# One more pair of weight chunks converted in place, and a planner that rests for two steps, in a banded attention with two feed-forward layers

## The chip, the cores and the metric

The kernel runs on one core of one Trainium2 chip. The metric is the device time of one execution in microseconds (us), from several runs; the trace comes from one more, profiled execution. Engines are named as the profile names them: PE is the matmul engine (TensorE), DVE is VectorE, ACT is ScalarE, POOL is GpSimd, and SP is the engine that issues most of the DMAs.

## What is computed

Attention with a band mask on q, k, v of shape (4, 8, 576, 64), then two feed-forward layers on the 2304 tokens of 512 features that come out of it, all in float32:

```python
scores = where(mask, q @ k.T / 8, -1e9)          # 32 keys back; dilated by 4 for half of the heads
x = softmax(scores) @ v                          # as (2304, 512)
h = x @ w_in                                     # 512 -> 2048
g = where(h > 0, h, exp(min(h, 0)) - 1)
x = g @ w_out                                    # 2048 -> 512
out = ((x @ w_a) * (x @ w_b)) @ w2_out           # 512 -> 1536 -> 512
```

The weights reach the chip as 64-bit floats, seen as pairs of 32-bit words, so every weight has to be put together on the chip before a matmul can use it.

## The kernel before

**Tiles and steps.** The tokens stand in six tiles of 384. The first layer's 2048 hidden features are 16 columns f of 128. A *step* is one pair (tile t, column f); `STEPS1` lists the 96 of them: steps 0 to 6 are tile 0 with f = 0 to 6, steps 7 to 22 are tile 1 with f = 0 to 15, steps 23 to 31 are tile 0 with f = 7 to 15, and from step 32 tiles 2 to 5 follow, 16 steps each. Behind the steps comes the second layer, by Strassen-like products (`ab_step`, lines L974 and L1290).

**One step** s issues `h1_mm(s)`: 12 matmuls into the PSUM tile ps_h (L525; two such buffers), then on ACT a Relu (L546) and an Exp (L547); `h1_g(s)`: on DVE the join of both (L552), which frees ps_h for step s + 2, on ACT the high part of g (L536), on POOL its low part (L537); and `y1_mm(s - 2)`: 12 matmuls from g into four tiles ps_y (L571). Every float32 product is three passes of a high and a low part. When a tile's last column is done (step 6 for tile 0's first part, step 22 for tile 1), two ACT copies (L608) and two DVE copies (L606) empty ps_y and free it for the next tile. The attention of a later tile runs between the steps, in slots of its own: scores (L474), softmax (L490, L356, L360, L369, L370), transposes (L499) with ACT copies (L502), values (L514), and the split of the result into x (ACT L462, DVE L463). Scores, transposes and values share two PSUM buffers, ps_a.

**Weights of the first layer.** Column f needs the chunk ("1i", f) for h1 and ("1o", f) for y1, 128 x 512 weights each. A chunk is a DMA of 512 KB into a buffer wraw (four of them), and then: ACT L252 (high word), ACT L257 (low word), DVE L262, L267 and L270 (clamp, join, sign), ACT L278 (high part), DVE L297 or L854 (low part). There are two ways to issue this. `w_convert` does it in place ("inline"), a pair of chunks at a time, in slot "C" of one step; `w_load` issues the DMAs a step ahead. This is done for the columns f below `SPLIT` = 7. For the rest, `chunk_ops` puts the same operations into a list that the planner works off.

**The planner.** `tick()` is called twice per step, once in slot "C" and once as a half-step in the next step's slot "A0". Each tick adds an allowance per engine (`ROOM1` for its first 32 ticks: 1.8 us of DVE and 1.4 of ACT; then `ROOM`) and issues from the head of the list whatever is ready: its inputs were issued enough ticks ago, a buffer is free, and the allowance is not used up. Behind the chunks of the first layer stand the second layer's weights in the same list (`unit_ops`: assembly, sums L917, low parts L901, high parts L278, and DMAs to DRAM, L829). Which instruction stands where on an engine is then settled by the tile framework from the order of issue and its dependences; at run time each engine works through its own list in order.

The place where the two ways part, and the loop that sets the ticks:

```python
    for f in range(NF1):                                             # L1394
        ...
        if f >= SPLIT:                                               # L1397
            for k in ks[::-1]:
                chunk_ops(k)
            continue
        ...
        at_step(st, "C", w_convert, ks, "w", ON1)                    # L1404
...
    for st in range(C1, NS1 - 3):                                    # L1461; C1 = 7
        same = st < C0 or STEPS1[st - 2][0] == STEPS1[st - 1][0]
        at_step(st, "C" if same else "C2", tick)
        at_step(st + 1, "A0", tick, True)
```

Of the kernel before, what the change touches and what calls it, by code (L numbers as in the profile page):

```python
# [36 lines left out]
SPLIT = 7  # L37
# [25 lines left out]
ON0, ON1 = "AAV", "AAV"  # L63
# [152 lines left out]
def banded_attention_two_ffn(ctx: ExitStack, tc: tile.TileContext, ins, out):  # L216
# [626 lines left out]
    def chunk_ops(key):  # L843

        at = {}
        x = assembly(at)(key)

        def hi():
            at["to"] = pools["wb"].tile([128, 2, 512], F32R, tag="w", name="w")
            part_hi("A", at["to"][:, 0, :], at["t", key])  # L850

        def lo():
            w = w_sb[key] = at["to"]
            V.tensor_tensor(w[:, 1, :], at["t", key], f32(w[:, 0, :]), op=SUB)  # L854

        give("wraw", x)
        give("wt", Op("V", 512, lo, Op("A", 512, hi, x)))
# [464 lines left out]
    def at_step(step, slot, fn, *args):  # L1322
        todo.setdefault((step, slot), []).append((fn, args))
# [70 lines left out]
    for f in range(NF1):  # L1394
        st = f
        ks = [("1o", f)] + ([("1i", f + 2)] if f + 2 < NF1 else [])
        if f >= SPLIT:  # L1397
            for k in ks[::-1]:
                chunk_ops(k)
            continue  # L1400
        for k in ks:
            if k != ("1o", 0):
                at_step(max(0, st - 1), "B" if f else "L", w_load, k)
        at_step(st, "C", w_convert, ks, "w", ON1)  # L1404


    def held(fn, *args):
# [51 lines left out]
    for j in range(FP):  # L1459
        unit_ops(j)  # L1460
    for st in range(C1, NS1 - 3):  # L1461
        same = st < C0 or STEPS1[st - 2][0] == STEPS1[st - 1][0]
        at_step(st, "C" if same else "C2", tick)
        at_step(st + 1, "A0", tick, True)
# [113 lines left out]
```

## Time and profile before

| | us |
|---|---|
| median of 3 runs | 916.57 (915.07 to 921.31) |
| profiled execution | 915.85 |
| its span, first to last instruction | 914.0 |
| mean granted clock of PE | 0.998 of full speed |

Idle time in the span counts only on the engine that sets the end. In a timeline row the first number is the start in us from the span's beginning and the second the duration of the merged instructions; "[0.42 <-DVE el L552]" says that the engine sat idle for 0.42 us before it, until line L552 on DVE released it. In a waits row stand the sum in us, how many waits, and the longest. Matmul ends are modelled, so for PE the distance from one start to the next is the better measure than a duration.

### The profile page before, as it was taken

Reading aid. Unit: us, or ns where it says so; the run is one execution under the profiler, and the core shown is the slowest. Engines: PE = TensorE matmul, PEld = TensorE weight load, DVE = VectorE, ACT = ScalarE, POOL = GpSimd, SP = SyncE. Lnnn points to the kernel's source line nnn. Section 1 sums busy time; section 2 is a strip of 40 time slices with the busy share of each in tenths; the row PEclk is TensorE's granted clock in tenths of the full one; section 3 lists DMA queues with packets and bytes.
Section 4 is the critical chain, followed back from the end, with each engine's and each line's share of the span. In section 5 each row is a group of like instructions: output and inputs, shape, how many; then the busy total and the mean of one; then the engine's idle time right before and its main releaser. Section 6 shows DMA issues by size and latency. Waiting matters only on the chain.

```text
span 914.0 us, 17034 instructions
## 1 busy us (share of the span) xinstructions
PE 897.7 (98%) x6157; PEld 862.7 (94%) x6157; DVE 657.5 (72%) x1147; ACT 522.7 (57%) x1328; POOL 284.1 (31%) x260
## 2 busy tenths in 40 slices
PE   9999999999999999999999999999999999999998
PEld 6789988899999999999999999999999999999998
DVE  6898899759767777767876366688746688656666
ACT  6898788777777777876766343325443225343231
POOL 2323234333333333332323122222622222522233
PEclk9999999999999999999999999999999999999999
DMA  9764344648656455645997588675787754687722
GB/s 286 227 225 164 134 150 144 219 144 271 198 178 217 157 176 192 207 160 184 327 356 270 179 289 281 226 259 179 233 329 252 252 196 144 226 311 242 243 69 70
DMA packets 75860, 195.80 MB, mean 214 GB/s; under 512 B 8288, under 2 KB 22240, under 8 KB 75776
## 3 DMA queue, kind: packets, MB, share of 16 engines
q1 hardware_dynamic: 63680, 175.70, 57.0%
q10 hardware_dynamic: 12096, 19.01, 5.7%
q8 instruction: 49, 0.80, 0.3%
q14 instruction: 35, 0.29, 0.1%
HBM read 151.16 MB, written 43.52 MB: 213 GB/s over the span
## 4 chain that ended last, share of the span: by engine, by line
PE 72%; DVE 4%; issue 1%; ACT 0%; DVEq 0%
PE ps_h L974 27%; PE ps_y L571 14%; PE ps_h L525 14%; PE ps_o L1290 13%; PE ps_s L474 1%; PE ps_v L514 1%; PE ps_o L1150 1%; PE ps_t L499 1%; DVE u L1082 0%; DVE yt L733 0%; DVE acc L1313 0%; DVE u L1064 0%; DVE y L703 0%; DVE wraw L917 0%; DVE u L1046 0%
## 5 line engine op out<-in xcount | busy, mean ns | idle before, releaser
L974 PE MATMUL ps_h<-y,w 128*128 128x384 f32 x1512 | 293.0, 337 | 1.5 <-DVE el L1029 1.1
L974 PEld LDWEIGHTS ps_h<-y,w 128*128 128x128 f32 x1512 | 256.0, 188 | 4.4 <-DVE el L1029 2.0
L571 PE MATMUL ps_y<-g,w 128*128 128x384 f32 x1152 | 224.4, 341 | 2.0 <-ACT w L278 1.4
L525 PE MATMUL ps_h<-x,w 128*128 128x384 f32 x1152 | 222.9, 340 | 3.6 <-DVE el L552 2.1
L525 PEld LDWEIGHTS ps_h<-x,w 128*128 128x128 f32 x1152 | 199.0, 188 | 9.0 <-DVE el L552 3.2
L571 PEld LDWEIGHTS ps_y<-g,w 128*128 128x128 f32 x1152 | 200.4, 189 | 6.3 <-ACT w L278 1.8
L537 POOL TENSOR_TENSOR g<-el,g 128x384 fp32r<-128x384 f32 x96 | 116.6, 1215 | 276.7 <-ACT g L536 230.7
L1290 PE MATMUL ps_o<-w,g 128*128 128x256 f32 x1071 | 153.4, 281 | 0.4 <-ACT g L1090 0.4
L1290 PEld LDWEIGHTS ps_o<-w,g 128*128 128x128 f32 x1071 | 147.2, 188 | 0.9 <-ACT g L1090 0.9
L552 DVE SCALAR_TENSOR_TENSOR el<-el,ps_h 128x384 f32<-128x384 f32 x96 | 53.0, 552 | 80.4 <-ACT el L547 78.0
L1016 POOL TENSOR_TENSOR g<-el,g 128x384 fp32r<-128x384 f32 x34 | 38.4, 1131 | 121.7 <-ACT g L1015 106.8
L1313 DVE TENSOR_TENSOR acc<-acc,ps_o 128x512 f32<-128x512 f32 (+1 forms) x77 | 49.7, 645 | 34.3 <-PE ps_o L1290 34.0
L546 ACT ACTIVATE el<-ps_h 128x384 f32<-128x384 f32 x96 | 46.5, 485 | 38.4 <-PE ps_h L525 33.6
L267 DVE SCALAR_TENSOR_TENSOR wt<-wt,wraw 128x512 uint32<-128x512 uint32 x68 | 62.2, 919 | 3.8 <-ACT wraw L257 1.4
L270 DVE SCALAR_TENSOR_TENSOR wt<-wraw,wt 128x512 uint32<-128x512 uint32 x68 | 60.5, 895 | 0.8
L536 ACT ACTIVATE g<-el 128x384 fp32r<-128x384 f32 x96 | 49.6, 516 | 16.7 <-DVE el L552 16.6
L370 POOL TENSOR_TENSOR e<-e,rs 96x512 f32<-96x512 f32 (+2 forms) x40 | 40.7, 1018 | 47.1 <-DVE rs L369 47.1
L547 ACT ACTIVATE el<-el 128x384 f32<-128x384 f32 x96 | 50.2, 523 | 1.7
L360 ACT ACTIVATE e<-e,nm 96x128 f32<-96x128 f32 x128 | 49.8, 391 | 0.7
L257 ACT ACTIVATE wraw<-wraw 128x512 uint32<-128x512 uint32 x68 | 45.1, 669 | 5.4 <-DMA wraw<-in_w2o 2.8
L1064 DVE TENSOR_TENSOR u<-ps_h,u 128x384 f32<-128x384 f32 x36 | 20.0, 557 | 39.0 <-PE ps_h L974 39.0
L1025 ACT COPY el<-ps_h 128x384 f32<-128x384 f32 x36 | 17.2, 478 | 50.4 <-PE ps_h L974 50.4
(111 smaller groups left out, 1084.0 us busy)
## 6 DMA issues: line engine op xcount, KB each, us to landing
w<-w2P_o SPq DMA_DIRECT2D x52, 512.0 KB, 5.6
w<-w2P_a SPq DMA_DIRECT2D x48, 512.0 KB, 4.5
w<-w2P_b SPq DMA_DIRECT2D x48, 512.0 KB, 4.4
wraw<-in_w1i SPq DMA_DIRECT2D x16, 512.0 KB, 4.1
wraw<-in_w1o SPq DMA_DIRECT2D x16, 512.0 KB, 3.5
wraw<-in_w2a SPq DMA_DIRECT2D x12, 512.0 KB, 3.6
wraw<-in_w2b SPq DMA_DIRECT2D x12, 512.0 KB, 3.6
wraw<-in_w2o SPq DMA_DIRECT2D x12, 512.0 KB, 3.8
```

The costliest lines, as they stand in the source:

```text
L267: V.scalar_tensor_tensor(t, t, 3, L, op0=ALU.logical_shift_left, op1=ALU.bitwise_or)
L270: V.scalar_tensor_tensor(t, H, 0x80000000, t, op0=ALU.bitwise_and, op1=ALU.bitwise_or)
L360: A.activation(e[:, i], sc[:, i], AF.Exp, bias=nm[:, i : i + 1], scale=scale, accum_out=sm[:, i : i + 1],)
L525: T.matmul(ps[:, :TB], w[:, wi, kc * 128 : (kc + 1) * 128], xs[kc][:, xi, :], start=(n == 0), stop=(n == 3 * KC - 1),)
L536: A.activation(g[:, 0, :], gf, AF.Copy)
L537: G.tensor_tensor(g[:, 1, :], gf, f32(g[:, 0, :]), op=ALU.subtract)
L547: last_e[0] = A.activation(e, e, AF.Exp, scale=-1.0)
L552: last_g[0] = V.scalar_tensor_tensor(e, e, -1.0, h_ps.pop(s)[:, :TB], op0=ALU.add, op1=ALU.max)
L571: T.matmul(y_ps[t][c][:, :TB], w[:, wi, c * 128 : (c + 1) * 128], g[:, gi, :], start=(first and n == 0), stop=(last and n == 2),)
L974: last_mm[0] = T.matmul(ps[:, :TB], w[:, wi, kc * 128 : (kc + 1) * 128], y2[S, yop][kc][:, xi, :], start=(start and n == 0), stop=(n == 5) ...
L1290: T.matmul(ps[:, 256 * n : 256 * n + 256], g[name][:, gi, i * 128 : (i + 1) * 128], w[:, wi, h, :], start=((first or not held) and n == m ...
L1313: V.tensor_tensor(a, a, ps[:, :n], op=ADD)
```

## The change

The condition that sends a column to the planner becomes `f > SPLIT`: the pair of column 7, chunks ("1o", 7) and ("1i", 9), is now converted inline in step 7, with its results in the buffer pool "wb" that the planner's chunks use; its DMAs are issued by `w_load` in step 6. The planner keeps its allowances and starts with the pair of column 8. It is not called at all for steps 23 and 24: two ticks and two half-steps fall away.

```diff
-        if f >= SPLIT:
+        if f > SPLIT:
             for k in ks[::-1]:
                 chunk_ops(k)
             continue
...
-        at_step(st, "C", w_convert, ks, "w", ON1)
+        at_step(st, "C", w_convert, ks, "w" if f < SPLIT else "wb", ON1)
...
     for st in range(C1, NS1 - 3):
+        if 23 <= st < 25:
+            continue
         same = st < C0 or STEPS1[st - 2][0] == STEPS1[st - 1][0]
```

DVE in steps 7 to 9, before. The first two rows belong to the pair of column 6; L463 finishes x of tile 1, L606 empties ps_y:

```order
L267 SCALAR_TENSOR_TENSOR wt<-wt,wraw 128x512 x2
L270 SCALAR_TENSOR_TENSOR wt<-wraw,wt 128x512 x2
L463 TENSOR_TENSOR x<-ps_v,x 128x4x96
L297 TENSOR_TENSOR w<-wt,w 128x512 x2
L552 SCALAR_TENSOR_TENSOR el<-el,ps_h 128x384
L606 COPY el<-ps_y 128x384
L552 SCALAR_TENSOR_TENSOR el<-el,ps_h 128x384
L606 COPY el<-ps_y 128x384
L552 SCALAR_TENSOR_TENSOR el<-el,ps_h 128x384
```

The same place now:

```order
L463 TENSOR_TENSOR x<-ps_v,x 128x4x96
L297 TENSOR_TENSOR w<-wt,w 128x512
L262 TENSOR_SCALAR wt<-wt 128x512
L297 TENSOR_TENSOR w<-wt,w 128x512
L262 TENSOR_SCALAR wt<-wt 128x512
L267 SCALAR_TENSOR_TENSOR wt<-wt,wraw 128x512
L552 SCALAR_TENSOR_TENSOR el<-el,ps_h 128x384
L267 SCALAR_TENSOR_TENSOR wt<-wt,wraw 128x512
L270 SCALAR_TENSOR_TENSOR wt<-wraw,wt 128x512 x2
L552 SCALAR_TENSOR_TENSOR el<-el,ps_h 128x384
L297 TENSOR_TENSOR w<-wt,w 128x512 x2
L606 COPY el<-ps_y 128x384 x2
```

The eight DVE operations of the new pair stand between L463 and the L606 copies, around the L552 of steps 7 and 8. From step 10 to step 21 the DVE list has the same operations in the same places as before, each with the next pair's chunk in it.

DVE from the L552 of step 23 to the first softmax operation (L490) of step 25, before; L901 and the conversion lines are the planner's:

```order
L552 SCALAR_TENSOR_TENSOR el<-el,ps_h 128x384
L262 TENSOR_SCALAR wt<-wt 128x512
L901 TENSOR_TENSOR wt<-wt,wraw 128x512
L267 SCALAR_TENSOR_TENSOR wt<-wt,wraw 128x512
L606 COPY el<-ps_y 128x384
L552 SCALAR_TENSOR_TENSOR el<-el,ps_h 128x384
L606 COPY el<-ps_y 128x384
L901 TENSOR_TENSOR wraw<-wraw 128x512
L901 TENSOR_TENSOR wt<-wt 128x256
L270 SCALAR_TENSOR_TENSOR wt<-wraw,wt 128x512
L463 TENSOR_TENSOR x<-ps_v,x 128x384
L490 TENSOR_TENSOR e<-ps_s,masks 96x512
```

The same stretch now:

```order
L552 SCALAR_TENSOR_TENSOR el<-el,ps_h 128x384
L606 COPY el<-ps_y 128x384
L552 SCALAR_TENSOR_TENSOR el<-el,ps_h 128x384
L606 COPY el<-ps_y 128x384
L463 TENSOR_TENSOR x<-ps_v,x 128x384
L490 TENSOR_TENSOR e<-ps_s,masks 96x512
```

Six planner operations ahead of L463 are gone from this stretch; the three L901 now stand ahead of the L552 of step 23.

ACT from the end of step 22's part to the L502 copies of step 23, before:

```order
L252 ACTIVATE wt<-wraw 128x512
L368 ACTIVATE rs<-sm 96x4
L546 ACTIVATE el<-ps_h 128x384
L278 ACTIVATE wraw<-wraw 128x512
L547 ACTIVATE el<-el 128x384
L829 DMA w2P_0_a<-wraw 128x512
L536 ACTIVATE g<-el 128x384
L502 COPY pt<-ps_t 128x384 x2
```

The same place now:

```order
L368 ACTIVATE rs<-sm 96x4
L829 DMA w2P_0_a<-wraw 128x512
L829 DMA w2Q__1954<-wt 128x256
L546 ACTIVATE el<-ps_h 128x384
L502 COPY pt<-ps_t 128x384
L547 ACTIVATE el<-el 128x384
L502 COPY pt<-ps_t 128x384
L278 ACTIVATE wt<-wraw 128x512
L536 ACTIVATE g<-el 128x384
```

The two L502 copies, which stood behind the L536 of step 23, now stand around its L547; one L252 and one L278 ahead of them are gone.

## Rows read from the trace of the kernel before

**Rows 1.** The page, part 1: busy us of the engine, share of the span, instructions

```profile
PE 897.7 (98%) x6157; PEld 862.7 (94%) x6157; DVE 657.5 (72%) x1147; ACT 522.7 (57%) x1328; POOL 284.1 (31%) x260
```

**Rows 2.** Who the matmul engine waited for, whole span: us in total, times, longest us

```profile
PE ps_h L525 <- DVE el L552: 2.1, 4, 1.1
PE ps_s L474 <- DVE x L463: 1.6, 1, 1.6
PE ps_v L514 <- ACT pt L502: 1.4, 1, 1.4
```

**Rows 3.** One stretch: length, busy us of PE, PEld, DVE, ACT, POOL, clock, DMA share, GB/s

```profile
160.00:170.00 10.00, 8.35 (x47) 7.86 (x48) 7.23 (x14) 5.61 (x20) 2.58 (x3) 0.83 0.70 227
```

**Rows 4.** Timeline of the matmul engine, steps 24 to 26: start, us, work [idle before, releaser]

```profile
150.16 2.38 PE L525 MATMUL ps_h<-x,w 128*128 128x384 f32 x12 [0.42 <-DVE el L552]
152.38 2.62 PE L571 MATMUL ps_y<-g,w 128*128 128x384 f32 x12
156.43 1.26 PE L514 MATMUL ps_v<-pt,v 128*64 128x96 f32 x16 [1.43 <-ACT pt L502]
157.61 2.35 PE L525 MATMUL ps_h<-x,w 128*128 128x384 f32 x12
161.99 1.60 PE L474 MATMUL ps_s<-qk 64*96 64x128 f32 x14 [1.65 <-DVE x L463]
163.52 3.43 PE L571 MATMUL ps_y<-g,w 128*128 128x384 f32 x12
166.79 2.24 PE L525 MATMUL ps_h<-x,w 128*128 128x384 f32 x12
168.87 2.24 PE L571 MATMUL ps_y<-g,w 128*128 128x384 f32 x12
```

**Rows 5.** Timeline of ScalarE, steps 23 to 25

```profile
155.91 0.84 ACT L502 COPY pt<-ps_t 128x384 f32<-128x384 f32 x2
159.13 0.48 ACT L462 ACTIVATE x<-ps_v 128x384 fp32r<-128x384 f32 x1
```

**Rows 6.** Timeline of VectorE, step 25

```profile
160.79 0.68 DVE L270 SCALAR_TENSOR_TENSOR wt<-wraw,wt 128x512 uint32<-128x512 uint32 x1
161.40 0.54 DVE L463 TENSOR_TENSOR x<-ps_v,x 128x384 fp32r<-128x384 f32 x1
```

**Rows 7.** Groups by line and form, 50 to 100 us: busy us, mean ns of one

```profile
L267 DVE SCALAR_TENSOR_TENSOR wt<-wt,wraw 128x512 uint32<-128x512 uint32 x15 | 13.6, 916 | 0.3
L270 DVE SCALAR_TENSOR_TENSOR wt<-wraw,wt 128x512 uint32<-128x512 uint32 x14 | 9.9, 721 | 0.0
L297 DVE TENSOR_TENSOR w<-wt,w 128x512 fp32r<-128x512 f32 x10 | 7.2, 754 | 0.0
L262 DVE TENSOR_SCALAR wt<-wt 128x512 f32<-128x512 f32 x13 | 6.2, 480 | 0.0
```

**Rows 8.** Timeline of VectorE, steps 7 to 9

```profile
73.38 2.10 DVE L267 SCALAR_TENSOR_TENSOR wt<-wt,wraw 128x512 uint32<-128x512 uint32 x2
79.29 0.55 DVE L552 SCALAR_TENSOR_TENSOR el<-el,ps_h 128x384 f32<-128x384 f32 x1 [0.66 <-ACT el L547]
80.85 0.56 DVE L552 SCALAR_TENSOR_TENSOR el<-el,ps_h 128x384 f32<-128x384 f32 x1 [0.50 <-ACT el L547]
84.30 0.56 DVE L552 SCALAR_TENSOR_TENSOR el<-el,ps_h 128x384 f32<-128x384 f32 x1 [2.15 <-ACT el L547]
```

**Rows 9.** Timeline of GpSimd, one row beside the first of rows 8

```profile
73.83 1.10 POOL L537 TENSOR_TENSOR g<-el,g 128x384 fp32r<-128x384 f32 x1 [2.33 <-ACT g L536]
```

**Rows 10.** Who waited for whom, 84 to 150 us

```profile
DVE el L552 <- ACT el L547: 7.7, 7, 2.2
ACT w L278 <- DVE wt L270: 5.5, 3, 2.0
```

**Rows 11.** Timeline of SyncE: the planner's load of chunk (1i, 9)

```profile
69.76 0.33 SPq L866 DMA_DIRECT2D wraw<-in_w1i  x1
```

**Rows 12.** DMA issues: line, engine, count, KB each, median us from issue to landing

```profile
wraw<-in_w1i SPq DMA_DIRECT2D x16, 512.0 KB, 4.1
```

## The prediction, made before the changed kernel ran

> **What bounds the kernel now.** I read the page's shares first: PE is busy for 897.7 of 914.0 us [rows 1]. Whatever other engines gain is worth at most the 914.0 - 897.7 = 16.3 us in which PE stands, plus what it loses at a low clock. So the list of what PE waited for comes next, and of it the waits that lie where the change is. Four waits for the L552 of DVE, 2.1 us together, fall in steps 17 to 24; one of 1.6 us for L463 and one of 1.4 us for L502 fall in steps 24 and 25 [rows 2]. The table of stretches, third, has one row at a granted clock below 1.00 in the whole middle of the kernel, 160 to 170 us, with 0.83 [rows 3]: right behind those two long waits a part of it ran at the lower level of 1.2 GHz. The timeline of PE, fourth, shows the place [rows 4]. The steps are found by counting the blocks of 12 matmuls: h1 of step 24 starts at 150.16, y1 of step 22 at 152.38, the attention values at 156.43 after 1.43 us of waiting for the L502 copies, h1 of step 25 at 157.61, the 14 score matmuls at 161.99 after 1.65 us of waiting for L463, y1 of step 23 at 163.52, h1 of step 26 at 166.79. From one h1 to the next but one this is 166.79 - 150.16 = 16.63 us. The next y1 starts 168.87 - 166.79 = 2.08 us later, which is what a block of 12 costs when nothing holds it; the y1 at 163.52 took 166.79 - 163.52 = 3.27. Here is the time that the change can win.
>
> What holds PE here is the queue on DVE and ACT. L463 at 161.40 starts when the planner's L270 at 160.79 lets it [rows 6], and it needs the ACT part L462, which was through at 159.13 + 0.48 = 159.61 [rows 5]: DVE is late by 1.8 us with planner work. L502 at 155.91 [rows 5] stands behind the L536 of step 23 on ACT.
>
> The steps before (9 to 22) are bound by the same two engines in another way: between 84 and 150 us DVE waits for the L547 of ACT for 7.7 us, seven times, and ACT for the L270 of DVE for 5.5 [rows 10]. The two wait for each other, while neither shows a wait for PE in that stretch. They run slower than PE and use up PE's lead until the L552 waits of [rows 2] begin. A delay put into this chain early therefore comes out at its end.
>
> **The change part by part.**
>
> *The inline pair.* DVE gets two each of L262, L267, L270 and L297. By the means 0.480, 0.916, 0.721 and 0.754 us [rows 7] that is 2 x 2.87 = 5.74 us; instructions in a row overlap by some 0.08, eight of them by 0.65, which leaves 5.1. The same pair was the planner's first and is not work added to the program: from step 10 to 21 the planner issues the same operations in the same places, one pair ahead. So the 5.1 us land in steps 7 to 9 alone. There DVE idled before its L552 for 0.66, 0.50 and 2.15 us [rows 8], 3.3 together, all behind L547. If the pair fills these, the chain leaves step 9 later by 5.1 - 3.3 = 1.8 us. The first part of the fill is not free, since ACT has the pair's six operations in the same steps; but ACT runs L546 and L547 of steps 7 and 8 back to back now, which gives some of it back. I take 1.5. Bounds: 0, if PE's lead at step 9 were never used up, and 5.1, if nothing of the idle time can be filled. PE itself waits a little in step 9, because the two L606 copies now follow the whole pair and the second part of y1 needs the bank that the first one empties; its list puts seven matmuls of h1 between, and what is left, under 1 us, is part of the same 1.5, for PE is held by the chain later anyway. The DMAs: `w_load` issues the pair's two loads where the planner's first two stood in SP's list (the first at 69.76 [rows 11]), for the buffers are freed by the same L270. The planner's next four loads keep their places too.
>
> One rule of the Trainium skill bears on these eight operations. [rows 8] has two L267 in a row taking 2.10 us at 73.38, against 0.916 for the mean, while POOL ran its L537 from 73.83 for 1.10 [rows 9]. "SBUF — State Buffer", section "Who interferes with whom", says that a DVE instruction with two SBUF inputs and a GpSimd instruction that reads SBUF exclude each other, and the second to start waits for the whole of the first. The trace agrees as far as one row can: 2.10 less two at the 0.721 of an L270 is 0.66 of the 1.10. Three of the pair's four kinds have two such inputs, and the L537 of steps 7 and 8 fall beside them; by the rule each can hold DVE up for the whole of its 1.10, so the term would be up to 1.5 + 2.2 = 3.7 and the sum 915.05. I keep 1.5: the means in [rows 7] already hold such meetings.
>
> *Steps 23 and 24 without the planner.* Ahead of L463 six planner operations leave DVE's list (L262, L901, L267, L901, L901, L270), and ahead of the L502 copies ACT loses more than it gets: the operations of the last chunk pair are one pair earlier everywhere, so from step 21 on seven conversions of some 0.55 us are gone there and three high parts came in, and the copies stand before the L536 of step 23. I put L502 at 153 us in place of 155.91, before y1 of step 22 ends (about 154.3): the wait of 1.43 goes. What is late next is L463: its ACT half L462 still follows the two L608 copies and L536 of step 24, and those follow the end of y1 of step 22. From L502 to L462 there were 159.13 - 155.91 = 3.2 us; it is L536 of step 23, some 1.1 us earlier, that leads this row, so I put L462 at 158.0 and L463 at 158.5. The scores' second bank is then free at about 158.6 to 159.0, when h1 of step 25 has been over since 157.2: PE still waits 1.4 us there.
>
> The stretch from h1 of step 24 to h1 of step 26, added up anew: four blocks of 12 at 2.08 = 8.3; the values 157.61 - 156.43 = 1.2; the scores, 163.52 - 161.99 = 1.5 for 14 partly at the low clock, 1.2 for all 16 at the full one; waits 0.2 for g in y1 and 1.4 for L463. That is 12.3 in place of 16.63, a gain of 4.3. In it the clock counts with 3.27 - 2.08 = 1.2 for the y1 and about 0.4 for the scores. I take it that the clock stays at 2.4 GHz, because one of two waits within 6 us goes, and the four waits in the L552 group, of up to 1.1 us [rows 2], left no stretch below 1.00. With the L552 of step 22 some 0.2 us earlier the gain is 4.5. Bounds: 0, if a new wait of the same length takes its place, and 4.5 + 1.4 = 5.9, if the L463 wait goes as well.
>
> *Behind step 25.* The planner is two steps behind where it would be, and one pair ahead: a pair takes it about two steps, so the second layer's weights keep their dates, the last conversions stand beside the same steps (92 and 93) in DVE's list, and the DMAs that fetch the weights only change places with neighbours. PE had no waits of note there, so I cost it at nothing; the cover is that L552 runs steps ahead of need once the first chunks are done. One operation could stop ACT: the first L257 of the next pair, which waits for a load of 4.1 us [rows 12] whose buffer is freed by DMAs to DRAM; it stands two steps ahead of the h1 that could feel it.
>
> *The sum.* 915.85 + 1.5 - 4.5 = 912.85 against the profiled execution. The median of the runs is 0.72 above that execution; the runs to come will scatter likewise, so I predict 913.5.
>
> **The rivals.**
>
> (a) *A larger gain.* The pair hides whole in the idle time of steps 7 to 9, and L463 comes early too: 915.85 - 5.9 = 910. For it: 3.3 us of idle time on DVE there. Against it: L462 cannot start before the copies of ps_y.
>
> (b) *Nothing moves.* The long waits change their names only: L502 comes early, but L462 takes the time up, or the pause still sends the clock down, which keeps 1.6 us; with 1.5 to 2 us for the pair and one of the two waits kept it comes out at 915.85 + 1.8 - 4.5 + 1.6 + 1.4 = 916.2. For it: both waits end in one ACT and DVE queue.
>
> (c) *Slower: the pair's load is late.* ACT's list now has L252 and L257 of the new pair ahead of L546 and L547 of step 7 and between the L278 of the pair before. At 73.8 us ACT arrives there; the load issued at 69.76 lands 4.1 us later [rows 11, 12], at 73.9, so there is no reserve. Every us by which it lands later stops ACT, then DVE's L297 and L552, and then h1 of step 9, and the chain behind carries it to step 22. With a load that is late by L us the result is 912.85 + L; from L = 3, a load of 7 us, the change loses, and with 5 (a load of 9 us) it is at 917.85. Against it: the loads before it took the same path in the same queue without a wait on ACT there.
>
> (d) *The planner is not relieved but deferred* and the second layer's weights come late, at 500 us and later. Each late fetch would cost PE a few us; against it stands the order of the lists. I would see 918 or more.
>
> **How the numbers follow.** My forecast 0.58, (a) 0.12, (b) 0.16, (c) 0.10, (d) 0.04. The forecast's own range is 911 to 916. (a) reaches down to 909 with the scatter of runs, (c) up to 918; 908.5 to 918 leaves out the far ends of (a), (c) and (d), under 2 in 10. One per cent, about what a measurement of this kernel tells from no change, is 9.2 us. Faster by over 1% would need more than the 5.9 us that stand to be won, 0.03; slower by over 1% needs a (c) or (d) at twice the size, 0.03; within 1% 0.94.
>
> **What would show it.** Right: no wait for L502 in front of the values in step 24, a wait for L463 of 1 to 1.5 us in step 25, no stretch of 160 to 170 us below a clock of 1.00, h1 of step 26 about 3 us earlier than 166.79, and h1 of step 24 1 to 2 us later than 150.16. Wrong in the first term: h1 of step 24 not later, or later by more than 3 us, with an ACT wait for the DMA of wraw at 74 us. Wrong in the second: a stretch from h1 of step 24 to that of step 26 of over 14 us. Wrong as a whole: new waits of PE behind 170 us.

## The result, and the profile after

| | before | after |
|---|---|---|
| median of the runs, us | 917.81 (915.07 to 921.31, 6 runs) | 927.02 (925.64 to 929.14, 6 runs) |
| ratio after to before | | 1.0106, 95% interval 1.0089 to 1.0123 |
| span of the profiled execution, us | 914.0 | 925.0 |

The changed kernel is slower by 1.06%, some 9 us. I had said 913.5, in a range from 908.5 to 918. The sign is wrong.

The shares of the engines on the page, which answer to [rows 1]:

```profile
PE 899.6 (97%) x6157; PEld 860.7 (93%) x6157; DVE 656.5 (71%) x1147; ACT 523.8 (57%) x1328; POOL 284.2 (31%) x260
```

No engine has more to do: DVE 656.5 against 657.5, ACT 523.8 against 522.7, and the counts are the same. PE's busy time grew by 1.9 us and the span by 11.0, so about 9 us are new standing time of PE. Who PE waited for over the whole span, which answers to [rows 2] (us in total, times, longest):

```profile
PE ps_h L525 <- DVE el L552: 3.0, 4, 1.1
PE ps_s L474 <- DVE x L463: 2.6, 2, 1.5
PE ps_v L514 <- DVE e L490: 2.2, 1, 2.2
PE ps_y L571 <- ACT el L608: 2.1, 2, 1.0
...
PE ps_t L499 <- DVE e L490: 1.2, 4, 0.5
...
PE ps_y L571 <- DVE el L606: 0.8, 1, 0.8
```

New in this list are the softmax operation L490, twice, and the copies L608 and L606 that empty the banks of y1 at the end of a tile. The place of the change itself went as I had it. PE's timeline from h1 of step 24 to h1 of step 26 in the kernel after answers to [rows 4] (start, us, work, idle time before and its releaser):

```profile
150.21 2.35 PE L525 MATMUL ps_h<-x,w 128*128 128x384 f32 x12
...
155.10 0.88 PE L514 MATMUL ps_v<-pt,v 128*64 128x96 f32 x16
155.91 2.37 PE L525 MATMUL ps_h<-x,w 128*128 128x384 f32 x12
...
159.81 1.11 PE L474 MATMUL ps_s<-qk 64*96 64x128 f32 x14 [1.14 <-DVE x L463]
160.85 2.39 PE L571 MATMUL ps_y<-g,w 128*128 128x384 f32 x12
163.07 2.28 PE L525 MATMUL ps_h<-x,w 128*128 128x384 f32 x12
```

The wait for L502 is gone, that for L463 is 1.14, and 163.07 - 150.21 = 12.86 us pass where it were 16.63. The table of stretches answers to [rows 3] and goes on to the end of the first layer (length, busy us of PE, PEld, DVE, ACT and POOL, clock, DMA share, GB/s), for the kernel after:

```profile
160.00:170.00 10.00, 10.00 (x70) 9.74 (x68) 7.20 (x14) 8.59 (x31) 3.48 (x4) 1.00 0.56 191
...
170.00:230.00 60.00, 55.34 (x405) 51.70 (x404) 42.44 (x72) 42.11 (x130) 19.31 (x17) 1.00 0.56 185
230.00:515.00 285.00, 278.69 (x1815) 265.75 (x1814) 198.03 (x340) 201.10 (x532) 87.76 (x79) 1.00 0.62 210
```

and the last two for the kernel before:

```profile
170.00:230.00 60.00, 59.89 (x434) 56.05 (x433) 44.66 (x79) 46.60 (x147) 21.46 (x20) 1.00 0.64 210
230.00:515.00 285.00, 285.00 (x1872) 276.74 (x1871) 201.83 (x345) 202.97 (x535) 89.72 (x79) 1.00 0.62 214
```

The long stretches hold the result. Before, PE stood 0.11 us in these 345. After, it stands 4.66 + 6.31 = 10.97, at an unchanged clock of 1.00. Nothing of it lies where the change was made.

The steps as a ruler show the same more finely. The table gives, for every kernel of this study, the start of h1 of a step on PE's timeline (the first of its 12 L525 matmuls) less the same in the kernel before, whose own are 150.16 (step 24), 166.79 (26), 230.49 (38) and 498.00 (95). Up to step 1 it is the scatter of the start.

```
h1 of step                 1     11     24     26     38     84     95
after                   1.14   1.97   0.05  -3.72   0.81   8.65  10.77
e1_inline_only          0.27   0.67  -0.80  -0.34   2.88  13.50  17.40
e2_rest_only            0.69   0.69   0.97  -2.49  -1.98  -0.49   2.38
e3_three_ticks         -0.09   0.71  -0.99  -4.59  -5.05  -5.05  -4.69
e4_three_steps          0.53   1.34  -0.31  -4.11  -4.15  -0.26   6.37
e5_rest4_only           0.73   0.77   0.91  -2.53  -3.08  -3.08   1.12
e6_five_ticks          -0.23   0.64  -1.20  -4.78  -4.35   0.28   5.08
e7_no_low               0.72   1.55  -0.29  -4.08  -2.27   2.38   6.34
e8_one_tick             0.54   1.32  -0.55  -4.10  -4.71  -1.11   0.69
e9_no_writes           -0.13   0.71  -1.16  -4.95  -0.76   8.30   8.30
e10_one_tick_back      -0.56   0.29  -1.57  -5.38   0.77   0.77   0.78
e11_before_less_one     0.22   0.23   0.25  -1.33  -1.16   5.47   6.50
e12_before_one_more    -0.45  -0.42  -0.42  -2.00  -1.72   2.85   5.88
```

The kernel after wins 3.77 between steps 24 and 26 and loses 14.49 from there to step 95, where nothing was edited. That is 3.5 more than the 10.97 us in which PE stands; the rest sits in blocks of matmuls that take longer without a gap in the rows.

Seen from close by, one such loss lies at the end of a tile, when the banks of y1 are emptied. PE in the kernel before, then in the kernel after:

```profile
289.54 2.34 PE L525 MATMUL ps_h<-x,w 128*128 128x384 f32 x12
291.72 2.25 PE L571 MATMUL ps_y<-g,w 128*128 128x384 f32 x12
```

```profile
290.81 2.34 PE L525 MATMUL ps_h<-x,w 128*128 128x384 f32 x12
294.17 2.75 PE L571 MATMUL ps_y<-g,w 128*128 128x384 f32 x12 [1.02 <-ACT el L608]
```

DVE between the two L490 of that softmax step, before:

```profile
283.39 0.68 DVE L490 TENSOR_TENSOR e<-ps_s,masks 96x512 f32<-96x512 f32 x1
284.00 0.68 DVE L901 TENSOR_TENSOR wt<-wt,wraw 128x512 fp32r<-128x512 f32 x1
284.60 0.68 DVE L356 TENSOR_REDUCE nm<-e 96x4 f32<-96x512 f32 x1
285.19 1.03 DVE L901 TENSOR_TENSOR wraw<-wraw 128x512 fp32r<-128x512 f32 x1
286.15 0.41 DVE L901 TENSOR_TENSOR wt<-wt 128x256 fp32r<-128x256 f32 x1
286.48 0.68 DVE L490 TENSOR_TENSOR e<-ps_s,masks 96x512 f32<-96x512 f32 x1
```

and after:

```profile
284.98 0.68 DVE L490 TENSOR_TENSOR e<-ps_s,masks 96x512 f32<-96x512 f32 x1
286.30 0.56 DVE L552 SCALAR_TENSOR_TENSOR el<-el,ps_h 128x384 f32<-128x384 f32 x1 [0.65 <-ACT el L547]
286.77 0.67 DVE L356 TENSOR_REDUCE nm<-e 96x4 f32<-96x512 f32 x1
287.37 0.41 DVE L262 TENSOR_SCALAR wt<-wt 128x512 f32<-128x512 f32 x1
287.70 1.51 DVE L901 TENSOR_TENSOR wt<-wt,wraw 128x512 fp32r<-128x512 f32 x1
289.14 0.68 DVE L267 SCALAR_TENSOR_TENSOR wt<-wt,wraw 128x512 uint32<-128x512 uint32 x1
289.74 0.68 DVE L490 TENSOR_TENSOR e<-ps_s,masks 96x512 f32<-96x512 f32 x1
```

From the first L490 to the second it took 3.09 us before and takes 4.76 now: L552, L356, L262, a long L901 and L267 stand between them, where L356 and three L901 stood. ACT's second group of exponentials (L360) waits for the second L490 and its L356, and the copies L608 stand around that group. ACT before:

```profile
288.44 0.46 ACT L608 COPY el<-ps_y 128x384 f32<-128x384 f32 x1
288.80 0.41 ACT L360 ACTIVATE e<-e,nm 96x128 f32<-96x128 f32 x1
...
290.86 0.47 ACT L608 COPY el<-ps_y 128x384 f32<-128x384 f32 x1
```

and after:

```profile
292.12 0.39 ACT L360 ACTIVATE e<-e,nm 96x128 f32<-96x128 f32 x1
...
293.66 0.46 ACT L608 COPY el<-ps_y 128x384 f32<-128x384 f32 x1
...
294.13 0.46 ACT L608 COPY el<-ps_y 128x384 f32<-128x384 f32 x1
```

The first copy stood ahead of the exponentials and ran at 288.44. Now both stand behind them, the first runs at 293.66, and PE waits for an empty bank until 294.17. The next end of a tile is alike: of the 7.84 us lost between steps 38 and 84, 4.57 lie in steps 49, 50, 65 and 66.

The longest single wait, 2.24 us, lies in step 29 and has another origin. ACT, DVE and PE in the kernel after:

```profile
184.26 0.66 ACT L257 ACTIVATE wraw<-wraw 128x512 uint32<-128x512 uint32 x1 [2.95 <-DMA wraw<-in_w2a]
185.88 0.56 DVE L552 SCALAR_TENSOR_TENSOR el<-el,ps_h 128x384 f32<-128x384 f32 x1 [4.59 <-ACT el L547]
187.09 0.88 PE L514 MATMUL ps_v<-pt,v 128*64 128x96 f32 x16 [2.24 <-DVE e L490]
```

ACT stands 2.95 us for a load of second-layer weights in front of the planner's L257. The L546 and L547 of step 29 stand behind it in ACT's list, so the L552 and then the L490 on DVE are late, and PE's value matmuls wait for them.

Nothing in the diff names these lines. The question for the experiments was what moved them.

### The profile page after: what moved, and what is told of

The parts are those of the page before. It is cut to its first block, busy times and chain, and to the rows that moved or that the text cites. A ratio compares the mean times of both kernels' runs of the same rounds, so it can differ in the third digit from the quotient of the medians.

```text
span 925.0 us, 16961 instructions
## 1 busy us (share of the span) xinstructions
PE 899.6 (97%) x6157; PEld 860.7 (93%) x6157; DVE 656.5 (71%) x1147; ACT 523.8 (57%) x1328; POOL 284.2 (31%) x260
## 4 chain that ended last, share of the span: by engine, by line
PE 51%; DVE 17%; DMA 9%; ACT 9%; issue 3%; POOL 0%; ACTq 0%; SPq 0%; DVEq 0%; POOLq 0%
PE ps_h L974 26%; PE ps_o L1290 13%; PE ps_y L571 5%; PE ps_h L525 4%; DVE wraw L917 2%; DVE wraw L901 2%; DVE wt L267 2%; ACT el L547 2%; DVE el L552 2%; DMA yt<-y 1%; DVE wt L901 1%; DVE nm L356 1%; ACT e L360 1%; DVE wt L270 1%; DVE e L490 1%
## 5 line engine op out<-in xcount | busy, mean ns | idle before, releaser
L525 PE MATMUL ps_h<-x,w 128*128 128x384 f32 x1152 | 223.4, 340 | 5.0 <-DVE el L552 3.0
L525 PEld LDWEIGHTS ps_h<-x,w 128*128 128x128 f32 x1152 | 198.8, 188 | 11.2 <-DVE el L552 5.1
L537 POOL TENSOR_TENSOR g<-el,g 128x384 fp32r<-128x384 f32 x96 | 115.5, 1203 | 279.7 <-ACT g L536 230.8
L552 DVE SCALAR_TENSOR_TENSOR el<-el,ps_h 128x384 f32<-128x384 f32 x96 | 52.8, 550 | 77.1 <-ACT el L547 76.2
L536 ACT ACTIVATE g<-el 128x384 fp32r<-128x384 f32 x96 | 50.1, 522 | 29.7 <-DVE el L552 29.4
L267 DVE SCALAR_TENSOR_TENSOR wt<-wt,wraw 128x512 uint32<-128x512 uint32 x68 | 55.8, 824 | 2.8 <-ACT wraw L257 1.5
L257 ACT ACTIVATE wraw<-wraw 128x512 uint32<-128x512 uint32 x68 | 44.9, 668 | 20.0 <-DMA wraw<-in_w2a 6.9
L252 ACT ACTIVATE wt<-wraw 128x512 f32<-128x512 f32 x68 | 45.2, 666 | 19.3 <-DMA w2R_o<-wt 4.0
L546 ACT ACTIVATE el<-ps_h 128x384 f32<-128x384 f32 x96 | 46.1, 481 | 14.7 <-PE ps_y L571 5.0
L270 DVE SCALAR_TENSOR_TENSOR wt<-wraw,wt 128x512 uint32<-128x512 uint32 x68 | 52.1, 773 | 0.4
L547 ACT ACTIVATE el<-el 128x384 f32<-128x384 f32 x96 | 50.1, 523 | 1.3
L360 ACT ACTIVATE e<-e,nm 96x128 f32<-96x128 f32 x128 | 49.8, 390 | 0.6
```

The costliest lines, as they stand in the source:

```text
L267: V.scalar_tensor_tensor(t, t, 3, L, op0=ALU.logical_shift_left, op1=ALU.bitwise_or)
L270: V.scalar_tensor_tensor(t, H, 0x80000000, t, op0=ALU.bitwise_and, op1=ALU.bitwise_or)
L360: A.activation(e[:, i], sc[:, i], AF.Exp, bias=nm[:, i : i + 1], scale=scale, accum_out=sm[:, i : i + 1],)
L525: T.matmul(ps[:, :TB], w[:, wi, kc * 128 : (kc + 1) * 128], xs[kc][:, xi, :], start=(n == 0), stop=(n == 3 * KC - 1),)
L536: A.activation(g[:, 0, :], gf, AF.Copy)
L537: G.tensor_tensor(g[:, 1, :], gf, f32(g[:, 0, :]), op=ALU.subtract)
```

## The experiments

The lists of the engines gave the first hint. Counting, for each L270 on DVE (one per chunk), the L552 ahead of it, the planner's work in the steady part stands like this:

```
before                 ... 34 35   38 39   42 43   46 47   50 51 ...
after                  ... 34 34   37 40   42 44   46 48   50 52 ...
e3_three_ticks         ... 33 34   36 39   42 43   46 47   50 51 ...
e10_one_tick_back      ... 34 34   37 39   42 43   46 47   50 51 ...
e11_before_less_one    ... 34 35   38 40   42 44   46 48   50 52 ...
```

An attention pair takes four steps, and so does a matrix of two chunks in the planner. Before, the two chunks of a matrix stand in neighbouring steps; after, they stand two apart. Three theories went into the first four runs. P: what decides is the place ("phase") of the planner's cycle in the four steps of an attention pair. Q: the four missing ticks are work that falls due later. R: the inline pair itself costs the time.

**e1, the inline pair alone.** The kernel after without its rest:

```diff
-        if 23 <= st < 25:
-            continue
```

> The pair of column 7 is converted inline, the planner rests nowhere. Theory P (phase): the loss behind 170 us comes from where the planner's work falls in the attention's cycle of four steps; here its list shows one chunk every two steps, as in the changed kernel, but two steps earlier in the cycle, so PE keeps new waits between 280 and 500 us and the time is 920 to 930, with the long waits of steps 24 and 25 still there. Theory Q (rest): the missing ticks make the second layer's weights late; then this kernel has no loss behind 170 us and comes to 916 to 918. Theory R (pair): the inline pair costs by itself, 927 or more.

Measured: 929.75 us (927.06 to 933.77), ratio 1.0146 (1.0118 to 1.0175). No tick is missing and yet it loses more than the kernel after, so Q falls. In step 24 the L502 wait is gone here too, but the one for L463 has become longer. PE in e1:

```profile
160.55 2.02 PE L474 MATMUL ps_s<-qk 64*96 64x128 f32 x14 [2.77 <-DVE x L463]
```

**e2, the rest alone.** The kernel after with the pair given back to the planner:

```diff
-        if f > SPLIT:
+        if f >= SPLIT:
```

> The planner rests in steps 23 and 24, the pair of column 7 stays with the planner. Theory P: its list shows two chunks back to back every four steps, as in the kernel before, but two steps off in the cycle; steps 24 and 25 lose their waits (h1 of step 26 at 161 to 164 us), and what is lost later decides the sign: 914 to 924. Theory Q: the missing ticks cost the full 9 us, about 927. Theory R: without the pair there is no loss, 912 to 914.

Measured: 918.38 us (917.58 to 921.35), ratio 1.0025 (1.0016 to 1.0034). Here L463 causes no wait, and L502 still does. PE in e2:

```profile
157.39 1.25 PE L514 MATMUL ps_v<-pt,v 128*64 128x96 f32 x16 [1.42 <-ACT pt L502]
```

So each half of the change acts on one of the two waits. The pair takes away that of L502; the rest shortens that of L463, from 1.65 us to none without the pair and from 2.77 to 1.14 with it.

**e3, three ticks left out in place of four.** The half-step issued in step 25 is put back:

```diff
-        if 23 <= st < 25:
-            continue
-        at_step(st, "C" if same else "C2", tick)
-        at_step(st + 1, "A0", tick, True)
+        if not 46 <= 2 * st < 49:
+            at_step(st, "C" if same else "C2", tick)
+        if not 46 <= 2 * st + 1 < 49:
+            at_step(st + 1, "A0", tick, True)
```

> The changed kernel with the last of the four ticks put back (the half-step of step 25). Theory P: the planner's list is from step 38 on that of the kernel before, chunk by chunk, so the waits between 280 and 500 us go and the gain of steps 24 and 25 (3.7 us at step 26) stays: 911 to 915. Theory Q: three of four ticks are still missing, about 924. Theory R: the pair is still there, 925 or more.

Measured: 911.65 us (911.31 to 914.76), ratio 0.9959 (0.9943 to 0.9974), against 927.02 for the kernel after, which leaves out one tick more. It has the pair, so R falls. From step 39 on its lists on DVE and ACT are those of before, word for word, and PE stands 0.07 us of the 285 from 230 to 515 us.

**e4, six ticks left out.** The rest lasts from step 23 to 25:

```diff
-        if 23 <= st < 25:
+        if 23 <= st < 26:
```

> The changed kernel with a rest of three steps instead of two (six ticks). Theory P: one chunk every two steps as in the changed kernel, one step later in the cycle; the time differs from the changed kernel's by several us, either way, 915 to 935. Theory Q: two more ticks are missing, so the loss grows by half, about 931. Theory R: the pair alone sets the time, 926 to 928.

Measured: 922.70 us (920.80 to 927.03), ratio 1.0073 (1.0049 to 1.0096). More rest, less loss than with four ticks left out; that again speaks for a phase and against an amount.

**e5, a whole cycle of rest without the pair.** The kernel after with `f >= SPLIT` and `23 <= st < 27`, eight ticks:

> No inline pair; the planner rests in steps 23 to 26, eight ticks, a whole one of its cycles of four steps. Behind step 40 its sign operations L270 stand in the same steps as before (42 and 43, 46 and 47, ...), each chunk one cycle of four steps later. Theory P (what decides is the planner's place in the four steps of an attention pair): no loss between steps 26 and 84, h1 of step 84 relative to before within 1 us of h1 of step 26, which is 3.5 to 5 us early; the last two chunks come in step 96 in place of 92 and 93 and may cost up to 3 us at the end; 911 to 915 us. Theory Q (missing ticks): eight are missing, twice those of the kernel after, so over 925. Theory R (the inline pair hurts, or the gain needs it): says here only that without the pair there is no more than the kernel e2 had, 918.

Measured: 917.41 us (915.29 to 919.57), ratio 1.0000 (0.9985 to 1.0015). The table of steps has -3.08 at step 38 and -3.08 at step 84: not a hundredth is lost in the phase of before, with twice the missing ticks. What was won goes in two other places: 4.20 between steps 84 and 95, where the last chunks come four steps later, and 2.8 - 1.12 = 1.7 behind step 95, by its span of 916.8. My 911 to 915 was too low by that; I had allowed 3 us for it.

**e6, five ticks, and e8, one tick.** As e3, with 51 and with 47 in place of 49:

> The inline pair, and five ticks left out (the kernel after leaves out four, e3 three). An odd number again, so the two chunks of a matrix stand in neighbouring steps, but all one step later than before (43 and 44, 47 and 48, ...). Theory P in its narrow form (only the place of before is good): 914 to 920 us, with a steady loss behind step 26 of 2 to 8 us. Theory P in its wide form (any place is good as long as the two chunks are neighbours, and only the spread one at a chunk every second step is bad): 910 to 914. Theory Q: over 925.

> The inline pair, and a single tick left out (first of step 23). Odd, so neighbouring steps, one step earlier than before (41 and 42, 45 and 46, ...). Theory P in its narrow form (only the place of before is good): a steady loss behind step 38 of 3 to 10 us. In its wide form (only the spread place is bad): under 1.5 us between steps 42 and 84. The waits of steps 24 and 25 largely stay with one tick left out, so the time is 916 to 920 us in the wide form and 919 to 926 in the narrow one.

Measured: e6 920.96 us (918.53 to 922.23), ratio 1.0037 (1.0022 to 1.0052); e8 915.70 us (914.24 to 916.94), ratio 0.9982 (0.9968 to 0.9997). Both have the two chunks in neighbouring steps and both lose, 4.63 and 3.60 us between steps 38 and 84. That is the narrow form of P. But they lose in different ways. In e8 all of it falls at the two ends of tiles, 1.80 us each in steps 50 and 66, where PE waits for the copies L608. In e6 PE does not stand at all between the h1 of steps 38 and 84, and the clock is 1.00:

```profile
226.14:452.52 226.38, 226.38 (x1508) 215.21 (x1507) 162.74 (x283) 165.76 (x460) 71.54 (x66) 1.00 0.57 191
```

What differs there is PE's own list. The values and the h1 of step 43, before:

```profile
254.54 0.88 PE L514 MATMUL ps_v<-pt,v 128*64 128x96 f32 x16
255.35 2.35 PE L525 MATMUL ps_h<-x,w 128*128 128x384 f32 x12
```

and in e6:

```profile
250.19 0.38 PE L514 MATMUL ps_v<-pt,v 128*64 128x96 f32 x2
250.50 0.44 PE L525 MATMUL ps_h<-x,w 128*128 128x384 f32 x1
250.87 0.87 PE L514 MATMUL ps_v<-pt,v 128*64 128x96 f32 x14
251.68 2.17 PE L525 MATMUL ps_h<-x,w 128*128 128x384 f32 x11
```

One matmul of h1 now stands among the values. From the first value matmul to the y1 that follows it takes 253.69 - 250.19 = 3.50 us, against 257.54 - 254.54 = 3.00 before. This comes in nine attention pairs, some 0.5 us each, and is the whole loss of e6 in these steps.

The total I gave e8 for the narrow form, 919 to 926, was too high, since I thought that one tick would leave the waits of steps 24 and 25 in place; it takes 13.08 us from h1 of step 24 to that of 26, where the others with the pair and a rest take 12.82 to 13.05.

**e7 and e9, what in the new place costs.** D: planner operations on DVE among the softmax steps. W: ACT standing for transfers in front of the planner's conversions, with L608, L546 and L502 behind it. ACT's waits in the kernel after from 166 to 515 us hold eleven such rows, 32.1 us together, the two largest:

```profile
ACT wraw L257 <- DMA wraw<-in_w2a: 6.9, 3, 3.0
ACT wraw L257 <- DMA wraw<-in_w2b: 5.5, 5, 2.5
```

where e3 has 1.2. In `parts`, e7 issues nothing for the low parts, and in `to_dram` e9 writes the first unit and R alone:

```diff
-                lambda: ENG[on[1]].tensor_tensor(src().bitcast(F32R), src(), hi(), op=SUB),
+                lambda: None,
```

```diff
+        if key[1] and key[0] != "R":
+            w2_dr[key] = w2_dr[(key[0], 0) + key[2:]]
+            n_done[key] = n_done.get(key, 0) + 1
+            return
```

> The kernel after with the low parts of the combined second-layer weights left out (every L901 of DVE; the whole values are written in their place, so the second layer's products come out different). ACT's work, the loads, the number and size of the writes and the planner's ticks stay. Theory D (in the new place the planner's DVE operations stand among the softmax steps L490 and L356 and the sums L463 and make PE wait): behind step 26 the loss of 14 us shrinks to 3 or less, total 911 to 917 us, even where ACT still waits for its buffers. Theory W (in the new place ACT stands waiting for transfers in front of the planner's L252 and L257, and its L608, L546 and L502 behind them are late): ACT's waits for DMA of some 35 us between 166 and 515 us stay over 20, and the total stays over 920.

> The kernel after without the writes to DRAM of the combined weights of all units but the first (R excepted); the later units' fetches read the first unit's weights, so the second layer comes out different. DVE's and ACT's operations and the planner's ticks stay; buffers are free when the last engine is through with them, and the loads behind the writes in SP's queue start sooner. Theory W: ACT's waits for DMA between 166 and 515 us, some 35 us, fall to under 10, and with them the loss behind step 26: total 911 to 917 us. Theory D: the waits of ACT fall too, but PE's waits for L490, L463 and L552 stay and the total stays over 920.

Measured: e7 920.66 us (919.60 to 924.20), ratio 1.0044 (1.0027 to 1.0061); e9 925.14 us (922.55 to 926.10), ratio 1.0080 (1.0056 to 1.0103). In e9 ACT's waits for transfers fall to six rows and 10.9 us, the longest of the groups 5.2, and the loss between steps 26 and 95 is still 13.25 us against 14.49. PE waits for the copies L608 for 4.4 us, against 2.1 in the kernel after. But the two executions do not have the same clock. The long stretches of e9:

```profile
170.00:230.00 60.00, 56.83 (x398) 53.55 (x399) 42.81 (x73) 42.04 (x130) 18.87 (x17) 0.97 0.53 168
230.00:515.00 285.00, 280.13 (x1818) 270.81 (x1818) 197.12 (x339) 199.66 (x532) 100.69 (x79) 0.99 0.39 127
```

PE stands 8.04 us here, against 10.97 in the kernel after, whose clock was 1.00 in both; e9 ran a part of them at 1.2 GHz. What the lower clock cost is, as an estimate from these rows, 60 x 0.03 + 285 x 0.01 = 4.7 us. So the writes are worth between 1 and some 6 us. e7 has one stretch at 0.83, from 370 to 380 us, by the same estimate 1.7 us of its loss.

W, which wanted 911 to 917 for e9, falls as the account of the whole, though e7 alone came out about where W had it (ACT's waits for transfers 18.8 us, total over 920). ACT's waits for transfers do not go with the loss either: between 166 and 515 us e4 has 44.7 us of them and loses 10.48 from step 26 to step 95, e6 has 8.9 and loses 9.86. But in single places W is what happens, as at 184.26, and e9 could not take that one away: it drops writes, and ACT waits there for a load, in e9 too for 2.79 us. D as I had put it falls as well: without any L901 the loss is 10.42 us, where 3 or less was expected. The low parts are worth 4 to 6 us of 14; L262, L267 and the four L917 stay in the steps in which the kernel after has them. One reservation holds for both: the order on DVE differs from that of the kernel after in 24 (e7) and 22 (e9) of 97 steps by neighbours that changed places, so these two runs weigh the parts only roughly.

**e10 and e11, the order exchanged.** The cleanest pair. e10 is the kernel after with one tick more, e11 the kernel before with one tick less, both at step 38:

```diff
+        if st == 38:
+            at_step(st, "C", tick)
```

```diff
-        at_step(st, "C" if same else "C2", tick)
+        if st != 38:
+            at_step(st, "C" if same else "C2", tick)
```

From step 40 on, e10 has the lists of before on DVE and ACT and e11 those of after, word for word; up to there each has its own. SP's list of transfers is exchanged with them. PE's list from 200 us on and POOL's whole list are the same in all four kernels.

> The kernel after with one tick more at step 38: from step 39 on DVE's and ACT's orders are those of before, word for word; up to there they are those of after. Theory P: the loss stops at step 39. h1 of step 42, 0.8 us later than before in the kernel after, is 0 to 1 us later here, and h1 of steps 60, 76 and 92 stay within 1 us of that (after: 3.3, 6.5 and 10.4); 913 to 917 us. If the loss comes from what was done before step 38 (the pair, the missing ticks, the weights' dates): a loss of more than 4 us between steps 42 and 92, and over 920 us.

> The kernel before with a single tick left out, the first of step 38: no inline pair, no rest in steps 23 and 24. From step 39 on DVE's and ACT's orders are those of the kernel after, word for word. Theory P: nothing changes up to step 38, then the loss of the kernel after comes in: h1 of step 60 is 1.5 to 4 us later than before, of step 76 4 to 7 and of step 92 7 to 11; 923 to 928 us. If the loss comes from the pair or the rest: within 2 us of before, 914 to 918 us.

Measured: e10 916.85 us (915.87 to 918.44), ratio 1.0004 (0.9994 to 1.0015); e11 923.85 us (922.25 to 926.43), ratio 1.0085 (1.0058 to 1.0111). e10 is 0.77 behind at step 38 and 0.78 at step 95. From 230 to 515 us PE never stands in it:

```profile
230.00:515.00 285.00, 285.00 (x1872) 276.72 (x1871) 201.76 (x345) 202.48 (x536) 90.65 (x79) 1.00 0.63 215
```

e11 has neither the pair nor the rest, and it loses 7.66 us between steps 38 and 95, with the same 2.1 us in two waits of PE for L608 that the kernel after shows. At step 92 it is 6.50 late where 7 to 11 was expected, for it comes 1.16 early to step 38. One tick of some 170 makes a difference of 0.85%. So it is the order that the planner's phase sets on DVE, ACT and SP together that makes the loss; which of the three lists does how much, these runs do not tell.

**e12, one tick early.** The kernel before with the two lines that e10 adds:

> The kernel before with one tick more at step 38 and nothing else: the planner is one tick early from there on, the one phase of its cycle of eight ticks that no run so far has had (the others: on time 0 us lost between steps 38 and 84, three early 10.6, two early 3.6, and one to four ticks late 7.8 or 6.6, 4.6, 3.9, 1.5). Theory P: up to step 38 as before, then a steady loss, 2 to 9 us between the h1 of steps 38 and 84, the two L270 of a matrix two steps apart; 917 to 926 us. Rival: being late is what costs, and being early costs nothing if it is slight (the kernel three ticks early also had the long waits of steps 24 and 25): 0 to 1 us lost, 915 to 918 us.

Measured: 924.50 us (921.69 to 925.34), ratio 1.0091 (1.0072 to 1.0110); 4.57 us lost between steps 38 and 84. Being early is no better than being late.

With that all eight phases have run. The planner numbers its own ticks. By that number the kernel after issues the last L270 at 146, 151, 157, 159, 166 and 168, the kernel before at 149, 154, 160, 162, 169 and 171: the pair saves it three ticks. So a kernel's phase is the ticks left out, less three if it has the pair:

```
phase, ticks late     kernels            lost between h1 of steps 38 and 84, us     PE stands there, us
0 (or 8)              e3, e5, e10        0.00, 0.00, 0.00                          0.00, 0.00, 0.00
1                     after, e11         7.84, 6.63                                5.02, 4.16
2                     e6                 4.63                                      0.00
3                     e4                 3.89                                      2.04
4                     e2                 1.49                                      0.91
5 (three early)       e1                 10.62                                     6.62
6 (two early)         e8                 3.60                                      2.45
7 (one early)         e12                4.57                                      3.01
```

Three kernels of different make lose nothing at phase 0, and every other phase loses, though not all by the same waits. In e1 a part of the 10.62 is clock: 0.90 from 370 to 380 us and 0.76 from 380 to 390, by these figures some 3.4 us. The two L270 of a matrix are three ticks apart. If the first falls on a whole tick, the second is in the next step; if it falls on a half-step, the second is two steps on. That is why an odd shift spreads the chunks.

## Why the prediction was wrong

**The first term, +1.5 for the inline pair, had the wrong sign.** From step 1 to step 24 the nine kernels with the pair change against before by -0.84 to -1.09 us (the kernel after: 0.05 - 1.14), those without it (e2, e5, e11, e12) by 0.03 to 0.28. Up to step 11 the pair costs about 0.8 in eight of the nine (0.4 in e1), less than my 1.5, and by step 24 it has given back more than twice that. DVE's waits for ACT's L547 between 84 and 150 us, which were 7.7 in seven places [rows 10], are now

```profile
DVE el L552 <- ACT el L547: 2.9, 3, 1.4
```

and PE's waits for L552 in that stretch and up to step 24 fall from 2.1 us in four places to 1.1 in one. I had said: "A delay put into this chain early therefore comes out at its end." I counted what the pair put in, and not what the chain gains when every later chunk is a pair ahead: ACT's waits for L270 in the same stretch fell too, from 5.5 [rows 10] to 2.0. Nor are the lists from step 10 to step 21 quite those of before: DVE's differs behind the L552 of step 11, ACT's in steps 9 to 13. The larger value, 3.7, that I worked out beside it from the Trainium skill ("SBUF — State Buffer", section "Who interferes with whom") falls with it. The rule itself agrees with the trace: two L297 of the pair beside an L537 took 2.48 us at 83.73, 0.97 more than two at the mean of [rows 7], and the L537 beside its two L270 took 2.00 at 82.23 against the 1.10 of [rows 9]. These delays are in the 0.8 that the pair costs up to step 11, and at step 24 nothing of them is left.

**The second term, -4.5, was right in kind.** Measured 3.77, with the L502 wait gone, 1.14 for L463 where I had 1.4, and no stretch under a clock of 1.00. I had put the first L502 copy at 153 and L463 at 158.5. In the kernel after, which answers to [rows 5, 6], they start at 153.72 and 159.19, 0.7 us later than that.

Of the 3.77, 1.57 are less certain than I took them. e11 and e12 have the lists of before up to step 38 and the same two waits (1.43 and 1.65, to 0.01), but stay at a clock of 1.00 and need 15.05 and 15.06 us from h1 of step 24 to 26. The dip of [rows 3] is thus not in every execution, and the waits alone are worth 15.05 - 12.86 = 2.19.

**The step that failed was "Behind step 25".** It said: "a pair takes it about two steps, so the second layer's weights keep their dates", and "PE had no waits of note there, so I cost it at nothing; the cover is that L552 runs steps ahead of need". What I had put at nothing measured 14.49 us from step 26 to step 95. Three things in it were wrong. A pair takes the planner three ticks and not four, so four ticks left out make it one tick late. That the last L270 still stand in steps 92 and 93 is true, and it hides that every second chunk before them has moved by a step. And the cover was the wrong one. Of the waits that came, most are not for L552 but for L490, L463, L502, L606 and L608: of the 10.6 us that the list of PE's waits shows from 166 to 515 us, 8.7. In the two places shown they feed PE in the step in which they stand. The one kind of operation that I had named as able to stop ACT, an L257 that waits for a load, did stop it, for 2.95 us at 184.26. I had written that "it stands two steps ahead of the h1 that could feel it"; what felt it 2.8 us later were the value matmuls. That PE stood 0.11 us in 345 was no proof of slack. It was the state of one phase out of eight.

By the table of steps the span's 11.0 us are 1.14 at the start, -1.09 up to step 24, -3.77 up to step 26, 14.49 up to step 95 and 0.2 behind it.

My condition "wrong as a whole: new waits of PE behind 170 us" is what came. Of the rivals, (d) was nearest in sign and size ("918 or more", 0.04), but its mechanism is not what happened: it had the weights late at 500 us, while 8.60 of the 10.72 us between the start of h1 in step 24 and in step 95 are lost by step 84, and the second layer adds only 11.0 - 10.77 = 0.2 to the span. (c), the late load, did not occur: ACT shows no wait for a transfer at the pair's own L252 and L257, which ran from 74.93 to 79.5.

With the phase put right, the two terms stand as the trace has them. e3 is this change less one tick of rest, and at 911.65 us it is in the 911 to 916 that I gave for the forecast's own range, and faster than both kernels.

What stays open is how much each of the planner's operations costs in each wrong place. e7 puts the low parts at 4 to 6 of 14 us and e9 the writes at 1 to 6; the rest was not taken apart. Why the tile framework puts a matmul of h1 among the values in e6 was not looked into.

## What to carry to other kernels

When two periodic sequences share in-order engines, here an attention pair of four steps and a planner of eight ticks, an edit that shifts one against the other changes the order in every later period, not only where it was made. Compare the lists of the engines far behind the edit, that of PE among them, before costing that part at nothing; here 76 of the 97 steps on DVE read differently. Then try the neighbouring shifts, which cost one number each: between the best and the worst of the eight lay 10.6 us from step 38 to step 84. And read a lost microsecond where it falls: e6 lost 4.63 us with a PE that was busy all the time.

## What was not expected of the hardware

The same order of instructions with the same two waits (1.43 and 1.65 us within 6 us) was followed by a granted clock of 0.83 from 160 to 170 us in one execution [rows 3] and by 1.00 in two others (e11, e12). It cost 1.57 us. In the kernel after, a single wait of 2.24 us at 187 us left the clock at 1.00, while in e10 one of 2.10 us at 185 us was followed by this:

```profile
180.00:190.00 10.00, 7.90 (x59) 7.18 (x56) 3.86 (x7) 5.61 (x21) 2.43 (x3) 0.83 0.33 104
```

Whether a wait of some 2 us brings PE down from 2.4 to 1.2 GHz could not be read from its length alone, so a term of a sum that rests on such a dip is better taken from several executions. The runs on record show that much: of the 20 runs of the kernel before that were timed with e5, the two with a mean clock of 1.000 took 915.20 and 915.29 us, and the three with 0.996 took 917.24 to 920.70.
